# A key-weight transpose held behind VectorE's fills, the first x tiles turned one by one, and a last tile cut 336 and 112

## The chip, the cores and the metric

One core of a Trainium2 chip. The metric is the device time of one execution in microseconds (us). Ratios are the mean time of one kernel's fast runs over that of the other's fast runs of the same rounds, so they are not quite the ratio of the medians quoted beside them. A trace shows one execution: that of the kernel before took 156.45 us.

Engines: PE is TensorE, PEld its weight loads, DVE VectorE, ACT ScalarE, POOL GpSimd; SyncE only issues transfers, and its queue is SPq.

## The reference

```python
x = A_x                                        # 2048 x 448
g = sigmoid((x * gate_w).sum(-1, keepdims=True))
qkv = x @ wqkv                                 # 16 heads of 28
phi(z) = concat(softmax(z @ w_phi), softmax(-(z @ w_phi)))
a = (phi(q) @ (phi(k).T @ v)) / (phi(q) @ phi(k).sum(0) + 1e-6) @ wo
b = gelu(x @ w1 + b1) @ w2 + b2
out = g * a + (1 - g) * b
```

## The kernel before

The kernel folds `w_phi` into the key and query weights on chip. For that it loads both weights transposed (`WkT`, `WqT`), multiplies them by a block-diagonal `w_phi` (line 221), and keeps `Wpk` and `Wpq`. Later stages split the contraction into halves of 64 rows, so that two token blocks run side by side on PE; they need copies of x and of the weights with the halves exchanged (`xS`, `WqS`, `WkS`, `WvS`), made by on-chip transfers. Almost all transfers are issued by SyncE, in this order:

```python
nc.scalar.dma_start(x0, x[0:512, :]...)               # ACT's queue: first four x tiles
nc.sync.dma_start(gate[0:1, :], gate_w[None, :])
for c, eng in ((0, nc.sync), (1, nc.scalar), (2, nc.sync)):
    eng.dma_start(WvG[:, c, 0:D], ...)                # value weights
...
load_wT(WkT, D)                                       # DMA transposes
load_wT(WqT, 0)
load_x(1)
...
load_x(2)
swap_w(WqS, Wpq)
swap_x(0)
load_x(3)
swap_w(WkS, Wpk)
swap_x(1)
swap_w(WvS, WvG)
...                                                   # then w1, wo, w2
```

PE begins with seven dummy matmuls, turns the four x tiles of `x0`, and works through values, folded weights, keys and queries:

```python
dummies(7)
xp = [ps.tile([P, NC4, 256], BF16, ...) for _ in range(2)]
turn_x0(0, xp[0])      # tiles 0 and 1: 8 transposes, one copy to SBUF on VectorE
turn_gate()            # gate column of WvG
turn_x0(1, xp[1])      # tiles 2 and 3, copied by ScalarE
fill_bd()              # block-diagonal w_phi, VectorE
v_pair(0, on_act=True) # values of tiles 0 and 1
v_pair(1)
prep(WkT, wk_at, (1, 0, 1))
prep(WqT, wq_at, (1, 0, 0))
...                    # k_pair, q_pair, then k_two/v_two with the halves
```

The softmax here doesn't subtract the row's maximum and nothing guards it: scores larger than these inputs give would overflow.

## Time and profile before

| | us |
|---|---|
| median of the 6 runs beside the change | 156.52 (156.32 to 157.11) |
| span of the profiled run | 154.5 |
| PE busy | 150.1 (97%) |
| first key matmul starts | 11.03 |
| last matmul ends | 151.18 |

The prediction below reads most of the profile. A timeline line gives start, duration, engine, source line, operation and tiles; a bracket is the idle time just before it and what ended it. From the timeline of SyncE's queue, the last of the half exchanges:

```profile
23.90 0.73 SPq L368 DMA_DIRECT2D WvS<-WvG  x1
```

and from PE's, the weight load that goes with the first matmul reading it (that matmul also starts at 28.11), and the last matmuls of the kernel:

```profile
28.11 0.09 PEld L288 LDWEIGHTS <-xS 64*128 64x128 bf16 x1 [0.17 <-issue]
...
150.63 0.55 PE L489 MATMUL y<-wo_sb,oT 128*128 128x224 bf16 x4
```

WvS took 4.2 us to land, 23.90 + 4.2 = 28.1. The last matmul ends at 150.63 + 0.55 = 151.18, which is 123.07 us after that load.

### The profile page before, as it was taken

To read this page: it belongs to the slowest core of one execution; us is meant where nothing else is said; L and a number is where in the kernel's file an instruction comes from. 1 tells how busy PE (TensorE), PEld (TensorE's weight loads), DVE (VectorE), ACT (ScalarE), POOL (GpSimd) and SP (SyncE) were. 2 spreads that over 40 slices of the span, in tenths; PEclk is the share of its full clock that TensorE was granted. 3 is DMA by queue.
4 is the path that set the end of the run, shared out by engine and by line. 5 is a ranking of instruction groups with operands and counts; after the bars stand their busy time and mean duration, and the time that the engine had idled before them with its cause. 6 is when DMAs were issued, how large, how long until landed. Compare 5 with 4: busy or idle time off the path is not lost.

```text
span 154.5 us, 3184 instructions
## 1 busy us (share of the span) xinstructions
PE 150.1 (97%) x1302; PEld 84.7 (55%) x1302; DVE 83.1 (54%) x245; ACT 77.3 (50%) x92; POOL 33.2 (22%) x36
## 2 busy tenths in 40 slices
PE   7999999999999999999999999999999999999991
PEld 2775545566666854444444455555556555555580
DVE  3454999389891050000000059999977999977100
ACT  2569759998889527676767740111311111111121
POOL 7940589919775000000000000000000000000000
PEclk9999999999999999999999999999999999999999
DMA  4999999999993000000000001124332124327401
GB/s 153 223 224 152 210 237 254 219 222 219 221 353 124 4 0 4 0 0 4 0 0 0 4 0 34 34 43 93 93 93 64 40 64 97 87 73 40 121 30 30
DMA packets 28242, 14.91 MB, mean 97 GB/s; under 512 B 20034, under 2 KB 27844, under 8 KB 28228
## 3 DMA queue, kind: packets, MB, share of 16 engines
q1 hardware_dynamic: 27012, 14.06, 42.5%
q10 hardware_dynamic: 1152, 0.65, 1.5%
q8 instruction: 10, 0.16, 0.4%
q14 instruction: 4, 0.03, 0.0%
q0 software_dynamic: 64, 0.01, 0.0%
HBM read 6.11 MB, written 1.84 MB: 51 GB/s over the span
## 4 chain that ended last, share of the span: by engine, by line
PE 97%; ACT 0%; issue 0%; DVE 0%; ACTq 0%
PE hp L424 27%; PE y L483 27%; PE pq L304 8%; PE y L489 8%; PE nm L439 4%; PE v_ps L205 4%; PE pk L274 4%; PE v_ps L288 4%; PE pk L296 3%; PE acc L315 2%; PE warm_ps L351 2%; PE w_ps L221 1%; PE xp L334 1%; ACT res L492 0%; DVE w_sb L115 0%
## 5 line engine op out<-in xcount | busy, mean ns | idle before, releaser
L483 PE MATMUL y<-w_sb,gel 128*128 128x448 bf16 (+1 forms) x238 | 45.2, 341 | 0.0
L424 PE MATMUL hp<-xT,w_sb 64*128 64x512 bf16 x196 | 42.7, 376 | 0.0
L424 PE MATMUL hp<-xS,w_sb 64*128 64x512 bf16 x196 | 42.3, 376 | 0.0
L429 ACT ACTIVATE gel<-hp,b1T 128x1024 bf16<-128x1024 f32 x28 | 30.8, 1111 | 13.0 <-PE hp L424 13.0
L492 ACT ACTIVATE res<-y,ungate 128x448 bf16<-128x448 f32 (+1 forms) x17 | 10.4, 612 | 50.4 <-PE y L489 50.2
L483 PEld LDWEIGHTS <-gel 128*128 128x128 bf16 x238 | 23.1, 98 | 19.0
L424 PEld LDWEIGHTS <-w_sb 64*128 64x128 bf16 x392 | 20.6, 94 | 21.5
L265 POOL TENSOR_TENSOR phik<-phik,rec 128x1792 bf16<-128x1792 bf16 (+1 forms) x8 | 25.0, 3129 | 14.1 <-DVE rec L262 14.1
L444 DVE COPY st<-nm 128x32 f32<-128x32 f32 x32 | 4.5, 184 | 35.6 <-PE nm L439 35.6
L460 DVE TENSOR_TENSOR tmp<-nm,al 128x448 bf16<-128x448 f32 x32 | 18.4, 617 | 0.0
L260 DVE TENSOR_REDUCE sums<-phik 128x64 f32<-128x1792 bf16 x8 | 16.0, 2006 | 2.7 <-ACT phik L253 2.7
L489 PE MATMUL y<-wo_sb,oT 128*128 128x448 bf16 (+1 forms) x68 | 14.7, 341 | 0.0
L304 PE MATMUL pq<-xT,Wpq 64*128 64x512 bf16 x56 | 13.2, 376 | 0.0
L304 PE MATMUL pq<-xS,WqS 64*128 64x512 bf16 x56 | 11.5, 376 | 0.0
L193 DVE CAST vaug<-v_ps 128x896 bf16<-128x896 f32 x7 | 7.5, 1074 | 5.5 <-PE v_ps L288 3.2
L309 ACT ACTIVATE EqP<-pq 128x1024 bf16<-128x1024 f32 x8 | 8.4, 1049 | 3.5 <-PE pq L304 3.5
L310 ACT ACTIVATE EqN<-pq 128x1024 bf16<-128x1024 f32 x8 | 8.4, 1052 | 0.0
L252 ACT ACTIVATE phik<-pk 128x896 bf16<-128x896 f32 x8 | 7.6, 950 | 1.5 <-PE pk L274 1.5
L439 PE MATMUL nm<-KVbd,EqP 128*128 128x120 bf16 x64 | 8.3, 216 | 0.0
L439 PE MATMUL nm<-KVbd,EqN 128*128 128x120 bf16 x64 | 8.3, 216 | 0.0
L489 PEld LDWEIGHTS <-oT 128*128 128x128 bf16 x68 | 6.1, 98 | 3.3
L253 ACT ACTIVATE phik<-pk 128x896 bf16<-128x896 f32 x8 | 7.7, 958 | 0.0
(91 smaller groups left out, 148.1 us busy)
## 6 DMA issues: line engine op xcount, KB each, us to landing
w_sb<-in_B_w_dram SPq DMA_DIRECT2D x4, 784.0 KB, 14.2
out_dram<-res SPq DMA_DIRECT2D x15, 112.0 KB, 1.9
w_sb<-in_B_w_dram SPq DMA_DIRECT2D x1, 1568.0 KB, 16.1
xS<-xT SPq DMA_DIRECT2D x2, 256.0 KB, 4.0
oT<-in_A_x_dram ACTq DMA_DIRECT2D x1, 448.0 KB, 3.1
xS<-xT SPq DMA_DIRECT2D x2, 192.0 KB, 4.2
wo_sb<-in_A_wo_dram SPq DMA_DIRECT2D x1, 336.0 KB, 17.4
WqS<-Wpq SPq DMA_DIRECT2D x1, 256.0 KB, 4.3
```

What stands on the lines that cost most here:

```text
L260: nc.vector.reduce_sum(out=sums[:], in_=ph, axis=AX.X)
L265: eng.tensor_tensor(out=ph[:, lo:hi], in0=ph[:, lo:hi], in1=rec[:, lo:hi, :, None].to_broadcast([P, hi - lo, 2, DH]), op=ALU.mult)
L304: nc.tensor.matmul(pq[:, i, :], lhsT=w_half(Wpq, WqS, i, k)[:, g * P:(g + 1) * P], rhs=x_half(i, k, h), start=(k == 0), stop=(k == NK - 1))
L309: nc.scalar.activation(out=EqP[:, g, dst], in_=src, func=ACT.Exp)
L310: nc.scalar.activation(out=EqN[:, g, dst], in_=src, func=ACT.Exp, scale=-1.0)
L424: nc.tensor.matmul(hp[:, i, :], lhsT=w1_sb[i * HP:(i + 1) * HP, k, j * P:(j + 1) * P], rhs=x_half(i, k, h), start=(k == 0), stop=(k == NK ...
L429: nc.scalar.activation(out=gel[h][:, j, :], in_=hp[:].rearrange("p a b -> p (a b)"), func=ACT.Gelu_apprx_tanh, bias=b1T[:, j:j + 1])
L439: nc.tensor.matmul(nm[s][:, g * 2 * KW:(g + 1) * 2 * KW], lhsT=E[:, g, tok], rhs=KVbd[:, g, s, :], start=True, stop=True)
L460: nc.vector.tensor_tensor(out=tmp[:, s, :].rearrange("p (x h d) -> p x h d", x=NPR, h=2), in0=nmv[s][:, :, 0:PW].rearrange("p x (h d) -> p ...
L483: nc.tensor.matmul(y, lhsT=gel[t // 8][:, j, (t % 8) * P:(t % 8 + 1) * P], rhs=w2_sb[:, j, cols], start=(j == 0), stop=False)
L489: nc.tensor.matmul(y, lhsT=oT[:, c, tok], rhs=wo_sb[:, c, cols], start=False, stop=(c == NC4 - 1))
L492: nc.scalar.activation(out=res[:, cols], in_=y, func=ACT.Copy, scale=ungate[:, t:t + 1])
```

## The change

The intent, as the edits show it: make SyncE issue the key transpose only after VectorE's fills (one more of which is moved there from POOL), so that the loads of x0 and WvG have the transfer engines to themselves; start the first value tile as soon as its own x tile is turned; and make the last eviction and store shorter.

```diff
+    nc.vector.memset(phik[:].rearrange("p t x s w -> p (t x s) w")[:, :, PW:HP], 0.0)
+    nc.vector.memset(WkT[0:1, 0, 0:1], 0.0)
...
-    nc.gpsimd.memset(phik[:].rearrange("p t x s w -> p (t x s) w")[:, :, PW:HP], 0.0)
...
-    def v_pair(u, on_act=False, b1=False):
+    def v_pair(u, on_act=False, b1=False, between=None):
         for i in range(2):
             t = 2 * u + i
+            if i == 1 and between is not None:
+                between()
...
-    def turn_x0(m, tp):
-        for i in range(2):
+    def turn_x0(t0, n, on_act):
+        ...                                   # its own PSUM tile, n tiles at a time
+        for i in range(n):
...                                            # turn_gate now uses the dummies' PSUM tile
-    turn_x0(0, xp[0])
+    turn_x0(0, 1, False)
     turn_gate()
-    turn_x0(1, xp[1])
+    turn_x0(1, 1, False)
+    v_pair(0, on_act=True, between=lambda: turn_x0(2, 2, False))
     fill_bd()
-    v_pair(0, on_act=True)
     v_pair(1)
...
-    for cols in (slice(0, 224), slice(224, D)):
-        y = y_tile()
-        dense_out(y[:, 0:224], NT - 1, cols)
-        attn_out(y[:, 0:224], NT - 1, cols)
+    for cols in (slice(0, 336), slice(336, D)):
+        y = y_tile()[:, 0:cols.stop - cols.start]
+        dense_out(y, NT - 1, cols)
+        attn_out(y, NT - 1, cols)
```

The one-element fill of `WkT` computes nothing: the transpose writes the same element, so SyncE must wait until VectorE has passed it.

More of the change, by code (lines that the diff above doesn't have):

```diff
@@ L328, in kv_out @@
                     in1=mask[rows, None, :].to_broadcast([PW, NG, PW + 2]), op=ALU.mult)
-    def turn_x0(m, tp):
-        for i in range(2):
+    def turn_x0(t0, n, on_act):
+        turn[0] += 1
+        if turn[0] % 4 == 0:
+            tp = ps.tile([P, NC4, n * P], BF16, name="xp", tag="acc", bufs=1)
+        else:
+            tp = ps.tile([P, NC4, n * P], BF16, name="xp", tag="pair", bufs=3)
+        for i in range(n):
             for c in range(NC4):
                 lo = c * P if c < 3 else 320
-                nc.tensor.transpose(tp[:, c, i * P:(i + 1) * P], x0[:, 2 * m + i, lo:lo + P],
+                nc.tensor.transpose(tp[:, c, i * P:(i + 1) * P], x0[:, t0 + i, lo:lo + P],
                                     ident[:])
-        copy(m == 1, xT[:, :, m * 256:(m + 1) * 256], tp[:])
-    def turn_gate():
-        g_ps = four("g_ps")
-        for c in range(NC4):
-            lo = c * P if c < 3 else 320
-            nc.tensor.matmul(g_ps[:, 0, c:c + 1], lhsT=gate[:, lo:lo + P], rhs=ident[:, 0:1],
-                             start=True, stop=True)
-        for c in range(3):
-            nc.scalar.copy(out=WvG[:, c, D:D + 1], in_=g_ps[:, 0, c:c + 1])
-        nc.scalar.copy(out=WvG[HP:P, 3, D:D + 1], in_=g_ps[HP:P, 0, 3:4])
+        copy(on_act, xT[:, :, t0 * P:(t0 + n) * P], tp[:])
+    w_ps = four("warm_ps")
     def dummies(n):
-        w_ps = four("warm_ps")
         for _ in range(n):
@@ L352, in dummies, with turn_gate @@
                              start=True, stop=True)
+    def turn_gate():
+        for c in range(NC4):
+            lo = c * P if c < 3 else 320
+            nc.tensor.matmul(w_ps[:, 1, c:c + 1], lhsT=gate[:, lo:lo + P], rhs=ident[:, 0:1],
+                             start=True, stop=True)
+        for c in range(3):
+            nc.scalar.copy(out=WvG[:, c, D:D + 1], in_=w_ps[:, 1, c:c + 1])
+        nc.scalar.copy(out=WvG[HP:P, 3, D:D + 1], in_=w_ps[HP:P, 1, 3:4])
     dummies(7)
-    xp = [ps.tile([P, NC4, 256], BF16, name="xp", tag="pair", bufs=3) for _ in range(2)]
-    turn[0] += 2
-    turn_x0(0, xp[0])
+    turn_x0(0, 1, False)
     turn_gate()
-    turn_x0(1, xp[1])
+    turn_x0(1, 1, False)
+    v_pair(0, on_act=True, between=lambda: turn_x0(2, 2, False))
     fill_bd()
-    v_pair(0, on_act=True)
     v_pair(1)
```

## The prediction

> **What bounds the kernel now.** I read the page's engine table first, then the chain that ended last in order of time, then the waits, and last the timeline of each engine over the first 30 us, because every line of the change but one lies there.
>
> ```profile
> PE 150.1 (97%) x1302; PEld 84.7 (55%) x1302; DVE 83.1 (54%) x245; ACT 77.3 (50%) x92; POOL 33.2 (22%) x36
> ```
>
> TensorE is busy for 150.1 of 154.5 us. The chain agrees: from the first dummy matmul at 1.06 us to the last matmul at 151.19 it stays on PE. So the change can gain only what PE does not use well: small holes, columns streamed at half rate at the start, and the tail after the last matmul. Any hole it makes on PE before 30 us costs its full length, since PE afterwards has none to give back.
>
> The head of the chain:
>
> ```profile
> 1.06 3.17 PE warm_ps L351 x7
> 4.23 0.85 PE xp L334 x8
> 5.08 0.09 PE g_ps L342 x4
> 5.17 0.88 PE xp L334 x8
> 6.04 3.13 PE v_ps L205 x16
> 9.17 2.02 PE w_ps L221 x32
> 11.19 4.54 PE pk L274 x24
> ```
>
> One transpose of 128 columns takes 0.85 us / 8 = 106 ns, that is 1.2 columns per ns. One value matmul of 449 columns takes 3.13 / 16 = 196 ns, 2.3 columns per ns. So the clock doubled at about 6.0 us, inside the first value matmul (421 ns long in the timeline, against 354 for the others).
>
> The timeline of SyncE's queue is what the change touches most:
>
> ```profile
> 2.58 2.57 SPq L136 DMA_TRANSPOSE WkT<-in_A_wqkv_dram  x1
> 5.20 1.85 SPq L136 DMA_TRANSPOSE WqT<-in_A_wqkv_dram  x1
> 7.10 1.95 SPq L132 DMA_TRANSPOSE xT<-in_A_x_dram  x1
> 9.09 1.26 SPq L133 DMA_TRANSPOSE xT<-in_A_x_dram  x1
> 10.40 1.64 SPq L132 DMA_TRANSPOSE xT<-in_A_x_dram  x1
> 12.08 1.26 SPq L133 DMA_TRANSPOSE xT<-in_A_x_dram  x1
> 13.52 0.56 SPq L367 DMA_DIRECT2D WqS<-Wpq  x1
> 14.13 1.20 SPq L368 DMA_DIRECT2D WqS<-Wpq  x1
> 15.38 0.65 SPq L141 DMA_DIRECT2D xS<-xT  x1
> 16.14 0.60 SPq L142 DMA_DIRECT2D xS<-xT  x1
> ```
>
> Each issue starts where the one before ends: from 2.58 us on, SyncE issues without a rest, and the largest hole (0.18 us, at 13.34) is tiny. So this queue is a second serial chain. Does it touch PE? In two places at least. The weight loads of the query folding say
>
> ```profile
> 10.09 0.17 PEld L221 LDWEIGHTS <-WqT 128*128 128x128 bf16 x3 [0.15 <-DMA WqT<-in_A_wqkv_dram]
> ```
>
> and WqT, issued at 5.20 with 4.8 us to landing, lands at 10.0. The second is the first query matmul that reads xS:
>
> ```profile
> 20.25 0.09 PEld L304 LDWEIGHTS <-WqS 64*128 64x128 bf16 x1
> 20.67 0.09 PEld L304 LDWEIGHTS <-WqS 64*128 64x128 bf16 x1 [0.33 <-issue]
> ```
>
> The view blames "issue", but the L142 swap, issued at 16.14, has 4.5 us to landing: 20.64. So I take the wait as that landing's. A third: WvS, issued at 23.90 with 4.2 us to landing, lands at 28.1, and the first loads that need it start at 28.11 after a 0.17 us hole. SyncE's chain thus already runs level with PE, with no slack.
>
> **What the Trainium skill says.** "DMA: Bandwidth & Descriptors", Anatomy of one DMA: a semaphore wait happens on the issuing sequencer before dispatch, not in the DMA engines. That means a transpose made to wait for VectorE holds everything behind it on SyncE. The trace has such a wait already (SyncE's gate-row load waited 0.6 us for a VectorE fill). The same page's Rules for kernel authors advises issuing early and waiting late; the change does the opposite for WkT. "VectorE: DVE Perf Modes", Zero memsets can be issued as uint32: a memset costs a cycle per element whatever the type, and a zero fill may go as 32-bit words; the trace agrees, the 448-column fills on VectorE are listed as 224 uint32 at 0.245 us while the odd 449-column one stays bf16 at 0.43. "TensorE: Matmul & The Clock Gate", Part 1: the array starts at half rate and doubles after a busy window of about 3.4 us; the trace agrees in kind (the doubling came 4.9 us after the first matmul).
>
> **The change part by part.**
>
> *Constant fill.* The phik fill of 2048 bf16 (1.80 us) leaves POOL, whose next urgent work is at 17.3 us: worth nothing. On VectorE, as 1024 words: start to start, 224 words take 0.33 us (2.05 to 2.38) and 449 elements 0.52 (1.53 to 2.05), so 0.85 ns per element; estimate 0.33 + 800 x 0.85 ns = 1.0 us, 1.15 at a full 1.04 ns cycle. VectorE is idle from 2.62 to 5.12, so this costs it nothing.
>
> *WkT behind it.* The one-element fill of WkT follows at about 3.8 us, and SyncE may issue the transpose at about 4.0 in place of 2.58: 1.4 us later. WkT took 2.57 us to issue, the equal-sized WqT 1.85. If the extra 0.7 came from the loads of x0 and WvG then in flight, part of it vanishes; I take off 0.4. Shift of the SyncE chain: 1.0 us, between 0.5 and 1.5.
>
> *x0 tiles singly.* PE's amount of work is the same: 16 transposes, 4 gate matmuls, 16 value matmuls. By the trace: tile 0 turned 4.02 to 4.45, gate to 4.60, tile 1 to 4.98. VectorE copies tile 0 as soon as its pass drains, at about 4.70 (before: 5.12, 0.04 after the eighth transpose's end), for some 0.4 us (half of 0.69, plus a fixed part), so the first value tile may begin at about 5.15 in place of 5.87. But it runs at half rate until 6.0, and it needs WvG's last columns, which landed at about 5.65. Then 8 transposes run at full rate. Columns streamed before 6.0 are thus not more than before; the gain here is nil, less about 0.1 of bubble. Tiles 2 and 3 can be multiplied only after their copy (0.69 us behind the last transpose, estimate 7.7 to 7.9), where PE is free at about 7.5: another 0.2 us of hole. Sum: PE reaches WkT's folding 0.2 to 0.3 later, at 9.3.
>
> *Where it meets the SyncE chain.* WkT lands at 4.0 + 4.8 to 5.4 = 8.8 to 9.4: just about in time. WqT lands 1.0 later, at 11.0, where PE would want it at about 10.3. So a wait of about 0.7 us takes the place of 0.15, and the first key matmul moves from 11.03 to about 11.05 + 0.94 = 12.0. At 20.64 the xS landing moves by the same 1.0. PE, already 1.0 late, meets it without more loss. So the two delays do not add: the kernel loses the shift of the SyncE chain, 1.0 us.
>
> *Last tile.* 336 + 112 columns in place of 224 + 224. PE's time is equal: 36 matmuls at 224 columns take 96 ns each; 18 at 142 and 18 at 49 come to the same 3.45 us, as the 120-column matmuls of L439 run at 0.42 / 8 = 53 ns, so weight loads don't bind. The last eviction shrinks:
>
> ```profile
> 149.54 0.45 ACT L492 ACTIVATE res<-y,ungate 128x224 bf16<-128x224 f32 x1 [1.09 <-PE y L489]
> 151.27 0.45 ACT L492 ACTIVATE res<-y,ungate 128x224 bf16<-128x224 f32 x1 [1.28 <-PE y L489]
> ```
>
> 448 columns take 0.63, 224 take 0.45; so 112 take about 0.36: 0.09 us gained, and the last store, half as large, perhaps 0.05 more.
>
> Sum: 156.35 + 1.0 - 0.15 = 157.2; leaning slightly toward a smaller shift, **157.1 us**.
>
> **The rivals.** (1) *A true gain in the head:* delaying WkT frees the DMA engines for WvG, whose last piece the gate copies waited for (0.27 us), and the first value tile starts 0.7 us sooner. For it: the early start is real. Against: PE has no hole there to fill, so all it could win is the 0.15 at WqT, the 0.2 at 20.3 and the 0.1 at 28.1, and each of these hangs on SyncE, which is later. If the transposes behind WkT issue or land much faster than before, this gives 155.9 to 156.3. (2) *The transfers are the limit, not their issue:* the DMA share is near 1.0 from 2 us to 46 us. Then a later start that leaves room for other loads costs less than the shift: 156.5. Against: the share dips to 0.65 at 11 us and 0.58 at 15 us, and packets follow issues. (3) *The clock doubles at another time:* a hole in PE's first 6 us could postpone it by one window of 3.4 us, at half rate 1.7 us lost: 158.5 or more; little speaks for it, as the holes are 0.2 us. (4) *The strided phik fill isn't packed into words:* 2048 elements, about 2.0 us, WkT at 5.0, and 158.1.
>
> **Range and chances.** The shift of 0.5 to 1.5 gives 156.7 to 157.7; I widen it downward for rivals 1 and 2 and upward for 4: 156.2 to 158.0. Runs of the kernel before spread over 0.35 us. Slower by over 2% means 159.5, which needs rivals 3 and 4 together: 0.03. Faster by over 2% means 153.2, more than all holes together: 0.01. Within 2%: 0.96.
>
> **What would show it.** SyncE's WkT issue at about 4.0 us, every later issue about 1.0 later, PEld's wait for WqT near 0.7 us, the first L274 key matmul at about 12.0, the first xS query matmul at about 21.6, the last ACT eviction at 0.36 us. I'm wrong if the WkT issue shrinks by a microsecond, if PE's first key matmul is not later than 11.03, or if the first value matmul at about 5.15 already runs at full rate.

## The result, and the profile after

The changed kernel took 157.16 us (median of 6, 156.88 to 157.70) against 156.52 for the kernel before: ratio 1.004, interval 1.0016 to 1.0064. It is slower by 0.25 to 1.0 us, inside the 2% that counts as the same. A second session gave 1.002 (0.999 to 1.005).

VectorE's timeline shows the two added fills:

```profile
2.78 0.91 DVE L121 MEMSET phik<- 128x1024 uint32 x1 [0.16 <-issue]
3.64 0.06 DVE L122 MEMSET WkT<- 1x1 bf16 x1
```

SyncE's queue follows them:

```profile
3.73 1.71 SPq L138 DMA_TRANSPOSE WkT<-in_A_wqkv_dram  x1
5.49 2.74 SPq L138 DMA_TRANSPOSE WqT<-in_A_wqkv_dram  x1
8.27 1.50 SPq L134 DMA_TRANSPOSE xT<-in_A_x_dram  x1
...
16.34 0.65 SPq L143 DMA_DIRECT2D xS<-xT  x1
17.09 0.60 SPq L144 DMA_DIRECT2D xS<-xT  x1
...
24.93 0.75 SPq L373 DMA_DIRECT2D WvS<-WvG  x1
```

The transpose is issued 1.15 us later than before (3.73 against 2.58), the first xS exchange 0.96 later, the last WvS exchange 1.03 later. What PE's weight loads waited for:

```profile
5.85 0.34 PEld L208 LDWEIGHTS <-xT 128*128 128x128 bf16 x2 [0.42 <-DMA WvG<-in_A_wqkv_dram]
...
11.31 0.17 PEld L224 LDWEIGHTS <-WqT 128*128 128x128 bf16 x3 [0.51 <-DMA WqT<-in_A_wqkv_dram]
...
21.48 0.09 PEld L307 LDWEIGHTS <-Wpq 64*128 64x128 bf16 x1 [0.19 <-issue]
...
29.13 0.09 PEld L291 LDWEIGHTS <-xS 64*128 64x128 bf16 x1 [0.17 <-issue]
```

The wait for WqT grew from 0.15 to 0.51 us, and the load that sets the end moved from 28.11 to 29.13. The chain that ended last says the same of WqT; its head no longer stays on PE but goes through the transfer:

```profile
4.23 0.57 PE xp L342 x4
...
5.49 5.78 DMA WqT<-in_A_wqkv_dram
11.27 0.05 issue
11.32 1.10 PE w_ps L224 x16
12.42 4.54 PE pk L277 x24
```

The chain stops at WqT, but PE met two more landings after it, each 0.04 us before the matmul that reads the data: xS at 21.65 and WvS at 29.09. From the first key matmul to the first matmul that reads WvS, PE takes 16.64 to 16.65 us in the three traces where no landing holds it on the way (g_swaps_after, h_gate, i_before_gate). The kernel before took 17.08 (0.44 of waiting), the changed kernel 16.88 (0.24). So the first key matmul starts 1.22 us later, and 0.20 of that is won back from these waits.

The tail, from the timeline of the last microseconds:

```profile
151.40 0.54 ACT L497 ACTIVATE res<-y,ungate 128x336 bf16<-128x336 f32 x1 [1.93 <-PE y L494]
...
151.83 0.36 PE L494 MATMUL y<-wo_sb,oT 128*128 128x112 bf16 x4
152.28 0.35 ACT L497 ACTIVATE res<-y,ungate 128x112 bf16<-128x112 f32 x1 [0.34 <-PE y L494]
```

The last matmul ends at 152.19, 1.02 us later than before (unrounded). From there to the end of the span it is now 3.12 us, against 3.30. So the span grew by 1.02 - 0.18 = 0.84 us (154.48 to 155.32).

### The profile page after: what moved, and what is told of

Same layout as the page of the kernel before. It is cut to its first block, busy times and chain, and to the rows that moved or that the text cites. A ratio compares the mean times of both kernels' runs of the same rounds, so it can differ in the third digit from the quotient of the medians.

```text
span 155.3 us, 3185 instructions
## 1 busy us (share of the span) xinstructions
PE 150.8 (97%) x1302; PEld 83.7 (54%) x1302; DVE 84.8 (55%) x249; ACT 76.3 (49%) x91; POOL 31.3 (20%) x35
## 4 chain that ended last, share of the span: by engine, by line
PE 93%; DMA 4%; DVE 0%; ACT 0%; issue 0%; SPq 0%; ACTq 0%
PE hp L429 27%; PE y L488 27%; PE pq L307 8%; PE y L494 8%; PE nm L444 4%; PE pk L277 4%; DMA WqT<-in_A_wqkv_dram 4%; PE v_ps L291 4%; PE pk L299 3%; PE acc L318 2%; PE warm_ps L350 2%; PE v_ps L208 2%; PE w_ps L224 1%; PE xp L342 0%; DVE xT L194 0%; ACT res L497 0%
## 5 line engine op out<-in xcount | busy, mean ns | idle before, releaser
L488 PE MATMUL y<-w_sb,gel 128*128 128x448 bf16 (+2 forms) x238 | 45.2, 341 | 0.0
L497 ACT ACTIVATE res<-y,ungate 128x448 bf16<-128x448 f32 (+2 forms) x17 | 10.4, 611 | 50.3 <-PE y L494 50.2
L488 PEld LDWEIGHTS <-gel 128*128 128x128 bf16 x238 | 22.6, 98 | 19.6
L429 PEld LDWEIGHTS <-w_sb 64*128 64x128 bf16 x392 | 20.5, 94 | 21.6
L494 PE MATMUL y<-wo_sb,oT 128*128 128x448 bf16 (+2 forms) x68 | 14.7, 341 | 0.0
L307 PE MATMUL pq<-xS,WqS 64*128 64x512 bf16 x56 | 11.6, 376 | 0.0
L255 ACT ACTIVATE phik<-pk 128x896 bf16<-128x896 f32 x8 | 7.6, 953 | 1.8 <-PE pk L277 1.8
L208 PE MATMUL v_ps<-WvG,xT 128*128 128x449 bf16 x32 | 7.7, 382 | 0.0
```

The source lines that it names most:

```text
L208: nc.tensor.matmul(v_ps[:, i, 0:D + 1], lhsT=xT[:, c, t * P:(t + 1) * P], rhs=WvG[:, c, :], start=(c == 0), stop=(c == NC4 - 1))
L307: nc.tensor.matmul(pq[:, i, :], lhsT=w_half(Wpq, WqS, i, k)[:, g * P:(g + 1) * P], rhs=x_half(i, k, h), start=(k == 0), stop=(k == NK - 1))
L429: nc.tensor.matmul(hp[:, i, :], lhsT=w1_sb[i * HP:(i + 1) * HP, k, j * P:(j + 1) * P], rhs=x_half(i, k, h), start=(k == 0), stop=(k == NK ...
L488: nc.tensor.matmul(y, lhsT=gel[t // 8][:, j, (t % 8) * P:(t % 8 + 1) * P], rhs=w2_sb[:, j, cols], start=(j == 0), stop=False)
L494: nc.tensor.matmul(y, lhsT=oT[:, c, tok], rhs=wo_sb[:, c, cols], start=False, stop=(c == NC4 - 1))
L497: nc.scalar.activation(out=res[:, cols], in_=y, func=ACT.Copy, scale=ungate[:, t:t + 1])
```

## The experiments

Two theories were set against each other. The **queue theory**: the loss is the late start of SyncE's serial chain. The **tile-order theory**: it comes from turning the tiles singly, through holes and columns streamed at half rate. Each run was timed in 5 rounds beside the kernel before on the same chip, in three sessions: a_nowait to d_wait_double; the changed kernel's second time and e to g; a_again and h to j. Times in us; "WkT" and "WvS" are the issues of the key transpose and of the last WvS exchange, "end" is the end of the last matmul in the trace.

| run | median | before | ratio (95%) | WkT | WvS | end |
|---|---|---|---|---|---|---|
| kernel before | 156.52 | | | 2.58 | 23.90 | 151.18 |
| changed kernel | 157.16 | 156.52 | 1.0040 (1.0016 to 1.0064) | 3.73 | 24.93 | 152.19 |
| changed, second time | 157.35 | 156.81 | 1.0020 (0.9990 to 1.0050) | 3.72 | 25.29 | 152.59 |
| a_nowait | 156.09 | 156.98 | 0.9949 (0.9930 to 0.9969) | 2.56 | 24.01 | 151.32 |
| a_again | 156.34 | 156.63 | 0.9978 (0.9963 to 0.9994) | 2.57 | 24.04 | 151.30 |
| b_wait_only | 157.37 | 156.98 | 1.0034 (1.0009 to 1.0059) | 3.72 | 25.15 | 152.36 |
| c_tail_only | 156.61 | 156.98 | 0.9976 (0.9956 to 0.9996) | 2.57 | 24.42 | 151.64 |
| d_wait_double | 158.28 | 156.98 | 1.0075 (1.0050 to 1.0099) | 4.90 | 25.90 | 153.29 |
| e_order_only | 156.79 | 156.81 | 0.9996 (0.9968 to 1.0024) | 2.58 | 24.09 | 151.37 |
| f_swaps | 158.62 | 156.81 | 1.0078 (1.0039 to 1.0117) | 2.58 | by POOL | 153.29 |
| g_swaps_after | 160.61 | 156.81 | 1.0085 (1.0028 to 1.0142) | 3.73 | by POOL | 152.40 |
| h_gate | 160.31 | 156.63 | 1.0243 (1.0203 to 1.0282) | 1.74 | 26.80 | 154.73 |
| i_before_gate | 160.81 | 156.63 | 1.0265 (1.0243 to 1.0286) | 1.73 | 27.20 | 155.01 |
| j_after_gate | 158.73 | 156.63 | 1.0123 (1.0087 to 1.0159) | 3.73 | 24.78 | 152.19 |

### Taking the wait away: a_nowait and a_again

```diff
 (changed kernel)
-    nc.vector.memset(WkT[0:1, 0, 0:1], 0.0)
```

> The changed kernel without the one-element WkT fill, so that SyncE issues the key transpose at about 2.6 us again. Queue theory (the loss is the late SyncE chain): WqT lands near 10.0, the first key matmul starts at 11.1 to 11.5, the swaps issue as before, total 156.4 to 156.7, at least 0.4 us below the changed kernel. Tile-order theory (the loss is holes and half-rate columns around the single tiles): total stays at about 157.1.

> The changed kernel without the WkT fill, run again beside the next three. Expected 0.3 to 0.8 us under the kernel before (0.9949 the first time); WkT issue at 2.6 us, WvS swap issued at about 24.0.

From SyncE's timeline of a_nowait:

```profile
2.56 2.45 SPq L137 DMA_TRANSPOSE WkT<-in_A_wqkv_dram  x1
...
24.01 0.75 SPq L372 DMA_DIRECT2D WvS<-WvG  x1
```

Everything of the change but one fill is still there, and the loss is gone: the last matmul ends at 151.3 in both traces, 0.9 to 1.3 us earlier than in the two traces of the changed kernel. The wait on the key transpose makes the loss, as the queue theory has it. The runs were even faster than the kernel before, by 0.2 to 0.5%; the next runs say where that comes from.

### The wait alone: b_wait_only

```diff
 (kernel before)
+    nc.vector.memset(phik[:]...[:, :, PW:HP], 0.0)
+    nc.vector.memset(WkT[0:1, 0, 0:1], 0.0)
-    nc.gpsimd.memset(phik[:]...[:, :, PW:HP], 0.0)
```

> The kernel before with the phik fill on VectorE and the one-element WkT fill behind it, nothing else. Queue theory: WkT issue at 3.7 us, the later SyncE issues about 1.0 later, total 157.3 (the changed kernel's loss without the gain of its tail). Tile-order theory: 156.5, as before.

With the tile order and the tail of the kernel before, the two fills alone cost 0.34% (0.5 us), and the SyncE issues moved as in the changed kernel. The tile-order theory, which expected no loss, falls.

### The tail alone: c_tail_only

```diff
 (kernel before)
-    for cols in (slice(0, 224), slice(224, D)):
+    for cols in (slice(0, 336), slice(336, D)):
```

> The kernel before with the last tile in 336 and 112 columns, nothing else. Both theories: PE time unchanged, last eviction 0.36 in place of 0.45 us, total 0.1 to 0.15 us below the kernel before (156.4).

A gain of 0.24% (0.38 us, interval 0.06 to 0.70). The trace gives the tail's part: from the end of the last matmul to the end of the span 3.10 us, against 3.30, so 0.20 us.

### The tile order alone: e_order_only

```diff
 (kernel before)
-    turn_x0(0, xp[0])
+    turn_x0(0, 1, False)
     turn_gate()
-    turn_x0(1, xp[1])
+    turn_x0(1, 1, False)
+    v_pair(0, on_act=True, between=lambda: turn_x0(2, 2, False))
     fill_bd()
-    v_pair(0, on_act=True)
```

> The kernel before with the x0 tiles turned singly around the first value tile and nothing else (fill on POOL, no WkT wait, old tail). Queue theory: SyncE's issues stand where they stood, so the total is within 0.3 us of the kernel before. Tile-order theory in its favourable form (a_nowait was 0.8 us under the kernel before, the tail alone 0.4): 0.4 us faster than before. In its unfavourable form: 0.3 us or more slower.

Ratio 0.9996: no gain or loss of the tile order is seen; the interval leaves room for 0.5 us of gain or 0.4 of loss. The first value tile starts at 5.36 in place of 5.87, and the end of the last matmul is 151.37 against 151.18. So of the gain of a_nowait the tail is the only part that a run shows by itself; whether anything is left beyond it the scatter does not tell.

### The dose: d_wait_double

```diff
 (changed kernel)
     nc.vector.memset(phik[:]...[:, :, PW:HP], 0.0)
+    nc.vector.memset(phik[:]...[:, :, PW:HP], 0.0)
     nc.vector.memset(WkT[0:1, 0, 0:1], 0.0)
```

> The changed kernel with the phik fill issued twice ahead of the WkT fill: WkT issue at 4.6 in place of 3.7 us. Queue theory: the whole SyncE chain and the total move by a further 0.9 us, to 158.0. Tile-order theory: no change, 157.2.

The key transpose was issued at 4.90 (expected 4.6), 1.17 us later than in the changed kernel. From the chain that ended last:

```profile
25.90 4.28 DMA WvS<-WvG
30.18 0.04 issue
30.23 1.49 PE v_ps L292 x13
```

The last WvS exchange came 0.97 later and the last matmul 1.10 later. Over both steps together, from the kernel before, the transpose is 2.32 us later and WvS 2.00, so 0.86 of each microsecond arrives at the end of SyncE's chain. How the two steps share this is not known: in the second trace of the changed kernel WvS is at 25.29, 0.36 later than in the first. The cleanest comparison is with a_nowait, which has the same tile order and tail and was timed in the same session: 2.34 us later at the transpose, 1.97 later at the last matmul, and 158.28 against 156.09 us in the timed runs. What absorbs the rest no run tests. Here the chain that ended last itself goes through the WvS landing.

### The changed kernel again: after_again

> The changed kernel unchanged, beside the others on one chip. Queue theory: the ratio to the kernel before is again near 1.004, WqT's landing at about 11.3 us is the last wait of the head, and the last matmul ends 123.06 us after the first matmul that reads WvS, as in all six traces so far.

This run shows a thing by luck. PE's clock had doubled before the first transpose (they took 56 ns each from 4.1 us on), while in the first trace of the changed kernel it doubled at 7.1. PE therefore reached the folding of WkT 0.7 us earlier (9.16 against 9.87). The weight loads show what that was worth:

```profile
11.53 0.94 PEld L224 LDWEIGHTS <-WqT 128*128 128x128 bf16 x16 [1.44 <-DMA WqT<-in_A_wqkv_dram]
```

It waited 1.44 us for WqT in place of 0.51, and the execution took 157.42 us against 157.02. So the faster PE in the head gained nothing; it only waited longer. That it ended later goes with SyncE's chain, whose last WvS exchange came 0.36 later. The expectation had also named WqT's landing as the last wait of the head. It was not: the first matmul that reads WvS starts at 29.53, 0.04 after WvS landed.

### Relieving SyncE: f_swaps and g_swaps_after

```diff
 (c_tail_only, and the changed kernel)
-    swap_w(WqS, Wpq)
-    swap_x(0)
+    swap_w(WvS, WvG, nc.gpsimd)
+    swap_w(WqS, Wpq, nc.gpsimd)
+    swap_x(0, nc.gpsimd)
...
-    swap_w(WvS, WvG)
```

> The kernel before with the new tail, and the WvS, WqS and first xS swaps issued from POOL in place of SyncE. Queue theory: PE no longer waits at 20.6 us for xS nor at 28.1 for WvS; the last wait of the head is WqT at about 10.1 to 10.2 us, the first WvS matmul starts at about 27.8, and the total is 0.6 to 0.9 us under the kernel before. If PE itself set the pace of the head: no faster than the tail alone, 0.4 under.

> The changed kernel with the same three swaps issued from POOL. Queue theory: the changed kernel's head is set by WqT's landing at 11.3, which stands ahead of all swaps, so this gains nothing: within 0.3 us of the changed kernel. If the swaps were what the late key transpose hurt: 0.6 to 0.9 us faster than the changed kernel.

A miss. In f_swaps the issues left SyncE, but the transfers became slower. From its chain of waits, and from SyncE's timeline:

```profile
14.73 8.09 DMA xS<-xT
22.82 0.04 issue
22.86 6.19 PE pq L304 x55
```

```profile
18.23 4.29 SPq L133 DMA_TRANSPOSE xT<-in_A_x_dram  x1
```

The xS exchange issued from POOL took 8.1 us to land (5.6 in g_swaps_after), against 4.5 from SyncE in the kernel before, and a transpose issued beside it held SyncE for 4.29 us, against 1.26 to 1.88 for that line's transposes in the traces with the swaps on SyncE. PE stood still for 1.71 us until xS was there. So the issue times are not fixed costs: here they grew with POOL's transfers in flight. Whether the crowd did it or the way in which POOL issues, these runs do not separate. The first half of the queue theory (what lands late makes PE late) stands; its simple form (each issue costs a set time, so fewer issues make a shorter chain) does not. Of the timed runs of g_swaps_after four of six fell in the slow state, so its ratio rests on two, and its trace is of the fastest execution. This one (157.55 us) shows PE waiting 1.18 us for WqT and for no landing after it, as expected, and its last matmul ends at 152.40, between the two traces of the changed kernel (152.19 and 152.59). The timed runs I call inconclusive. In f_swaps two of six were slow.

### An earlier start: h_gate, i_before_gate, j_after_gate

```diff
 (a_nowait, the kernel before, and the changed kernel)
-    nc.sync.dma_start(gate[0:1, :], gate_w[None, :])
...
+    nc.gpsimd.dma_start(gate[0:1, :], gate_w[None, :])
     nc.gpsimd.dma_start(wphi[0:64, 3, :], wphi_rows[384:448, :])
```

> The same with the gate row loaded from POOL's queue, so that SyncE's first load no longer waits 0.6 us for a VectorE fill and SyncE issues one transfer fewer: WkT issue at 1.6 to 2.2 in place of 2.6. Queue theory: every later SyncE issue moves up by 0.4 to 1.0 us and the total drops by 0.3 to 0.5 (PE itself can take no more, it reaches WqT at about 10.2). If the chain is limited by the DMA engines and not by the issues: landings and total stay within 0.2 of a_again.

> The kernel before with the gate row from POOL's queue and nothing else. Queue theory: 0.3 to 0.6 us under the kernel before. DMA-limit theory: same as before.

> The changed kernel with the gate row from POOL's queue. WkT's issue still waits for VectorE until 3.7 us, so queue theory: SyncE's chain from WkT on does not move, total within 0.2 us of the changed kernel (ratio 1.002 to 1.004), although WvG lands earlier. If WvG or the gate row were the limit of the head: 0.4 us faster.

This was meant as the opposite dose, and it missed far in the other direction: 2.4 and 2.7% slower (six runs of h_gate, four of i_before_gate). In h_gate SyncE issued the WvG loads at 0.81, beside x0, and the key transpose at 1.74. From SyncE's timeline and PE's weight loads:

```profile
1.74 3.22 SPq L136 DMA_TRANSPOSE WkT<-in_A_wqkv_dram  x1
...
16.64 0.57 SPq L371 DMA_DIRECT2D WqS<-Wpq  x1
```

```profile
5.10 0.23 PEld L341 LDWEIGHTS <-oT 128*128 128x128 bf16 x4 [1.77 <-DMA oT<-in_A_x_dram]
...
8.41 0.10 PEld L207 LDWEIGHTS <-xT 128*128 128x128 bf16 x1 [1.18 <-DMA WvG<-in_A_wqkv_dram]
```

x0 arrived at 5.1 us in place of 4.0, and the last of WvG at 8.2 in place of 5.9. PE stood idle three times for about 0.9 us, and its clock, which had run at full rate for the first transposes (55 ns apart), was at half rate again from 8.7 us (107 ns apart) until about 11.6. In i_before_gate the transposes ran at half rate, and the full rate came at about 12.3. In j_after_gate, which differs from h_gate in the transpose's wait alone, x0 was nearly as late (PE starts on it at 4.89), but WvG with its gate columns was complete by 7.1. So two things add up in h_gate: the WvG loads beside x0, and the transpose beside WvG. The gate row from POOL was slow as well (4.65 us to land in j_after_gate, where PE waited 1.00 us for it). How much each of the three costs these runs do not tell. j_after_gate also missed its expectation in the timed runs: five fast ones (the sixth was slow) were 1.2% slower, and the profiled execution (157.27) was the fastest of them, so no trace shows what held the others back.

The gate runs also turn the dependence round. SyncE issued the last transpose ahead of the exchanges until 13.86, half a microsecond later than in the kernel before for all its earlier start, and then waited: the WqS exchange needs Wpq, which PE's late folding had not yet made. In the view of waits this is 2.6 us in h_gate and 2.8 in i_before_gate. When PE reached the first matmul that reads xS (24.28 in h_gate), xS had been there since 23.08. So in these two runs PE was late and held the queue, not the queue PE.

What h_gate against j_after_gate does show is that the intent of the change was not empty: a transpose in flight beside the first loads does harm them (the last of WvG at 8.2 against 6.5). At 2.58 us, where the kernel before has it, little of that is left (5.89, against 5.81 in the changed kernel).

### The best version

a_nowait, which is the changed kernel without the `WkT` fill, beats the kernel before in two sessions: ratios 0.9949 and 0.9978. That is 0.2 to 0.5%, inside the 2% that counts as the same. Against the changed kernel it was never timed side by side; the comparison goes by way of the kernel before (1.0040 and 1.0020).

## Why the prediction was right or wrong

It was right: 157.1 us foretold, 157.16 measured, and by the mechanism it named. That the totals agree to 0.06 us is luck: the step was foretold as 0.75 us and measured as 0.64 between the medians, and the base it was added to was 156.35, the median of three runs, where six runs gave 156.52. By its steps:

- *SyncE is a second serial chain, level with PE.* Right, and shown by b_wait_only and d_wait_double. But its rule that any hole on PE before 30 us costs its full length was too strict: PE had 0.44 us of waits for landings on the way, and 0.20 of the 1.22 us came back there.
- *The fills.* The phik fill was packed into 1024 words and took 0.86 us from start to start, not 1.0. The transpose was therefore issued at 3.73, not 4.0. Rival 4 (an unpacked fill) did not occur.
- *Shift of the chain, 1.0 us.* It was 0.96 to 1.03, but as 1.15 less some 0.15, not as 1.4 less 0.4: two errors that cancel. The reason given for taking 0.4 off is half right. The WkT issue did shrink, from 2.57 to 1.71 us (0.86, near the microsecond that the prediction had named as a sign of being wrong), but the next issue, WqT, grew from 1.85 to 2.74. The slow issue moved rather than vanished. The chain made up 0.45 us in the next transpose (1.95 to 1.50) and lost 0.28 of it in a WqS exchange (1.20 to 1.48). Why one of the first issues is slow stays open.
- *x0 tiles singly: no gain.* Right within the scatter, by e_order_only (0.9996). Its inner times were off: the first value tile began at 5.31 (foretold 5.15), PE's clock doubled at 7.1 and not at 6.0, and PE reached the folding of WkT at 9.87 and not 9.3. The error cost nothing, since the wait for WqT took it up. Had PE been the bound, the step would have been wrong by half a microsecond.
- *The two delays do not add.* Right: first key matmul at 12.25 (foretold 12.0), first xS query matmul at 21.69 (foretold 21.6).
- *Tail.* The last eviction took 0.35 us (foretold 0.36), and the tail shrank by 0.18 to 0.20 (foretold 0.15).
- *The sum.* The trace of the change has +1.02 - 0.18 = +0.84 us, the working had +0.85 before it leaned to 0.75. The medians differ by only 0.64; the scatter of the runs (0.8 us within each kernel) covers that.
- *Rivals.* Rival 1 (a gain from freeing the first loads) shows only as traces: the last columns of WvG landed about 0.1 us sooner, and no gain shows. Rival 2 (the transfers, not their issue, are the limit) would fit the part of the delay, 14 to 16%, that did not arrive, but no run tests that. f_swaps, where issues stretched with the load, speaks for it more than I gave it. Rival 3 (a clock doubled at another time) did happen, and was hidden by the wait.

## What to carry to other kernels

A wait put on one transfer of an in-order queue delays every transfer behind it; before adding it, follow the queue to the last thing that the busiest engine needs from it, here 20 us later. When two chains run level, a gain on one is lost in the wait for the other, and a loss on either is paid nearly in full. Such chains can also wait on each other: SyncE's queue fed PE here, until PE was so late (h_gate) that the queue stood waiting for what PE makes. The good place for a transfer can be narrow: in these runs the key transpose at 2.6 us was better than at 3.7 and 4.9, and the runs that pulled it to 1.7, along with other loads, were the worst.

## What the Trainium skill lacked or had wrong

- "DMA: Bandwidth & Descriptors", Issuing engines are not separate DMA queues, calls the time to initiate a transfer "usually small relative to the DMA itself". Here issues of transposes held SyncE for 1.26 to 2.74 us each in the kernel before and the changed kernel, a large share of the 3.6 to 5.8 us to landing, and up to 4.29 us with POOL's transfers in flight. No page gives a figure for an issue that lengthens so.
- The same page's Rules for kernel authors say that spreading transfers over issuing engines doesn't help bandwidth. They do not say that it can cost time: the xS exchange took 8.1 us (f_swaps) and 5.6 us (g_swaps_after) to land when issued from POOL, 4.5 from SyncE.
- "TensorE: Matmul & The Clock Gate", Part 1, gives the doubling a spread of 500 ns (and warns that the number of slow matmuls varies from run to run). In twelve of these traces, whose first 4 us on PE are alike, it came between about 4.1 and 7.1 us, that is 3.0 to 6.0 after the first matmul. In h_gate, where PE stood idle three times for about 0.9 us, it was undone and came again at about 11.6, and in i_before_gate it came at about 12.3. Part 4 says that the full rate doesn't engage for transposes; in a_nowait and after_again they started 56 ns apart, 2.3 columns per ns as in the value matmuls at full rate. Matmuls had gone before them, so whether transposes alone would bring the full rate on is not shown.
- "VectorE: DVE Perf Modes", Zero memsets can be issued as uint32: one cycle per element at the 0.96 GHz of its table would be 1.07 us for 1024 words. The fill took 0.86 us from start to start, and 0.91 in the timeline.
